# Own PSUM banks for the first k and q, V shifts on VectorE, a first FFN step in token halves, split output tiles and a halved last tile in a fused attention and FFN kernel

## The chip, the cores and the metric

The kernel runs on one core of one Trainium2 chip. The metric is the device time of one execution in microseconds (us), lower is better. The profiled span of one execution is 1.7 to 1.9 us shorter than the time that is reported for the same execution. "PE" is the tensor engine, "DVE" the vector engine, "ACT" the scalar engine, "POOL" is GpSimd, "SP" is SyncE. Work in PSUM is read by DVE or ACT; such a read-out to SBUF is called an eviction here.

## The reference, cut to what matters

```python
# q, k, v: [8 batches, 8 heads, 576 positions, 64], float32
scores = (q @ k.T) / 8, masked to a causal window of 64 positions
attn = softmax(scores) @ v                     # -> x: [4608 tokens, 512]
g = x @ w_gate; val = x @ w_val                # 512 -> 1536
out = (g * sigmoid(g) * val) @ w_out           # 1536 -> 512, float32
```

The 4608 tokens are 36 chunks of 128 for the attention and 9 blocks (c = 0 to 8) of 512 for the FFN. One FFN block is 12 groups F(c, f) (eight matmuls of 512 columns each) and 4 output tiles O(c, u) (twelve matmuls each).

## The kernel before: the parts that matter

A small recording layer takes the operations in program order and puts one semaphore wait where two engines depend on each other. Each engine runs its own operations strictly in program order. PSUM has eight banks: 0 to 3 for the FFN groups, 4 for output tiles, 5 to 7 for everything of the attention.

For chunks 4 to 11, k and q are transposed on PE and evicted by DVE and ACT (for later chunks a DMA transposes them):

```python
def T(self, n):
    ...                                # one bank: k in its first half, q in its second
    g.op("pe", pe, ..., writes=[bk])   # 8 transposes 128x128
    g.op("dve", lambda e: e.tensor_copy(kd, tb[:, 0]), reads=[bk], writes=[kT..., (bk, "k")])
    g.op("act", lambda e: e.activation(qz[0:64, :, 0, :], tb[0:64, 1], ACTF.Copy),
         reads=[bk, (bk, "k")], ...)   # low heads of q; waits for the k copy: same bank
    g.op("dve", lambda e: e.tensor_copy(qz[64:128, :, 1, :], tb[64:128, 1]), reads=[bk], ...)
```

An FFN group, which needs both ACT and DVE:

```python
def F(self, c, f):
    G, gk = self.bank("f"); V, vk = self.bank("f")
    g.op("pe", mm(G, self.Wg), ...)
    g.op("act", lambda e: e.activation(sig, G, ACTF.Tanh, scale=0.5), ...)     # 0.60 us
    g.op("pe", mm(V, self.Wv), ...)
    g.op("dve", ... uu = (sig + 1) * G ...)                                    # 0.69 us
    g.op("dve", ... hT = 0.5 * uu * V ...)                                     # 0.69 us
```

The program order of the first blocks, cut:

```python
self.first_loads(); self.init(); self.load_v(0); ...; W(0, 1); ...   # weights after V
self.first_casts(0); ...; self.first_T(0); self.first_T(1); ...      # chunks 0 to 3
for n in range(4):
    self.Sx(n, 1, True); self.AV(n, 0)       # scores + exp; attention output
for n in range(4):
    self.AV(n, 1)
    if n > 0: self.X(n - 1, "act")           # transpose of x, evicted by ACT
self.X(3, "act")
load(4); load(5); self.load_wo(0, 6); self.load_wo(6, 12)
for f in range(6): self.F(0, f)
self.T(4); self.F(0, 6); self.Sx(4, 0); self.F(0, 7); self.Sx(4, 1); self.T(5) ...
```

The softmax here doesn't subtract the row's maximum and nothing guards it: scores larger than these inputs give would overflow.

## Time and profile before

355.31 us, the median of 3 runs (354.79 to 355.55); the profiled span is 353.6 us.

| stage (boundaries on PE) | us | PE busy | DVE busy | what paces it |
|---|---|---|---|---|
| prologue, to the first FFN matmul | 25.83 | 12.45 | 17.49 | waits between PE, DVE and ACT |
| F(0,0) to F(0,5) | 10.4 | 10.2 | 7.2 | PE |
| T(4) to the first output tile | 16.01 | 14.50 | 14.21 | see below |
| output tiles of block 0 | 16.15 | 15.07 | 9.22 | short waits |
| FFN block 1 | 29.30 | 27.22 | 25.43 | see below |
| the rest | 255.9 | 249.2 | 153.6 | PE, full |

The first two lines of the page give the span and each engine's busy time with its share:

```profile
span 353.6 us, 6112 instructions
PE 328.6 (93%) x2298; PEld 173.1 (49%) x2336; DVE 227.1 (64%) x484; ACT 140.8 (40%) x236; POOL 123.9 (35%) x163
```

The view of waits, PE alone. Each line: who waited, for what, us in total, how often, the longest. These are idle times of PE as the profile counts them, from the modelled end of the matmul before:

```profile
PE ps L316 <- ACT c L306: 7.6, 1, 7.6
PE ps L424 <- DVE nmask L274: 3.1, 1, 3.1
PE ps L509 <- DVE xT L484: 1.9, 2, 1.4
PE ps L532 <- DVE hT L519: 1.3, 1, 1.3
...
PE ps L532 <- DVE rc L462: 1.0, 1, 1.0
PE ps L509 <- ACT xT L486: 0.9, 1, 0.9
```

The reader sees a prologue that waits for the first cast (L306) and for `nmask` (a tile of large negative numbers that a matmul adds to the first scores to mask them), a wait at the end of FFN block 1 (`xT`), and one before the very last output tiles (`hT`, the tanh and the two DVE steps of the last group).

The windows view gives busy us (and number of instructions) of each engine in a stretch; the two stretches are "T(4) to the first output tile" and "FFN block 1":

```profile
core 0: us, PE busy (x) PEld busy (x) DVE busy (x) ACT busy (x) POOL busy (x), PEclk, DMA share, GB/s
36.21:52.22 16.01, 14.50 (x123) 8.19 (x125) 14.21 (x31) 6.92 (x12) 5.87 (x7) 1.00 1.81 188
68.37:97.67 29.30, 27.22 (x220) 14.99 (x225) 25.43 (x56) 12.89 (x22) 15.14 (x19) 1.00 1.50 152
```

DVE is busy 89% and 87% of these stretches, ACT 43% and 44%. The timeline of DVE around T(4) says something more exact (start, length, what, and the idle time before it with what ended it):

```profile
36.88 0.69 DVE L519 SCALAR_TENSOR_TENSOR hT<-uu,ps 128x512 bf16<-128x512 bf16 x1
37.49 0.42 DVE L387 COPY kT<-ps 128x512 bf16<-128x512 bf16 x1
37.94 0.43 DVE L390 COPY qz<-ps 64x512 bf16<-64x512 bf16 x1
39.05 0.69 DVE L517 SCALAR_TENSOR_TENSOR uu<-sig,ps 128x512 bf16<-128x512 bf16 x1 [0.68 <-ACT sig L515]
```

And ACT at the same time:

```profile
37.94 0.59 ACT L388 ACTIVATE qz<-ps 64x512 bf16<-64x512 bf16 x1 [1.81 <-DVE kT L387]
38.43 0.58 ACT L515 ACTIVATE sig<-ps 128x512 bf16<-128x512 f32 x1
```

ACT first waits 1.81 us for DVE's k copy, then evicts its half of q, then does the tanh, and DVE idles 0.68 us for that tanh.

### The profile page before, as it was taken

To read this page: it belongs to the slowest core of one execution; us is meant where nothing else is said; L and a number is where in the kernel's file an instruction comes from. 1 tells how busy PE (TensorE), PEld (TensorE's weight loads), DVE (VectorE), ACT (ScalarE), POOL (GpSimd) and SP (SyncE) were. 2 spreads that over 40 slices of the span, in tenths; PEclk is the share of its full clock that TensorE was granted. 3 is DMA by queue.
4 is the path that set the end of the run, shared out by engine and by line. 5 is a ranking of instruction groups with operands and counts; after the bars stand their busy time and mean duration, and the time that the engine had idled before them with its cause. 6 is when DMAs were issued, how large, how long until landed. Compare 5 with 4: busy or idle time off the path is not lost.

```text
span 353.6 us, 6112 instructions
## 1 busy us (share of the span) xinstructions
PE 328.6 (93%) x2298; PEld 173.1 (49%) x2336; DVE 227.1 (64%) x484; ACT 140.8 (40%) x236; POOL 123.9 (35%) x163
## 2 busy tenths in 40 slices
PE   1669989999899999999999999999999999999985
PEld 1654545555445555554555455545555555444432
DVE  6677795488956666666666666666666666655510
ACT  2463535454434444444444444444444444232222
POOL 8985517835643245424331437243100000000000
PEclk9999999999999999999999999999999999999999
DMA  8999999999989999999999999999944411100012
GB/s 238 195 208 172 219 160 209 196 165 156 126 62 149 162 157 152 153 158 154 156 153 159 162 141 155 154 152 150 170 117 113 104 45 46 45 30 32 30 59 89
DMA packets 178045, 48.17 MB, mean 136 GB/s; under 512 B 160160, under 2 KB 173408, under 8 KB 178016
## 3 DMA queue, kind: packets, MB, share of 16 engines
q0 software_dynamic: 113584, 17.84, 70.6%
q1 hardware_dynamic: 63376, 28.90, 41.0%
q10 hardware_dynamic: 1056, 1.05, 0.9%
q8 instruction: 18, 0.29, 0.3%
q14 instruction: 11, 0.09, 0.1%
HBM read 37.75 MB, written 9.44 MB: 133 GB/s over the span
## 4 chain that ended last, share of the span: by engine, by line
PE 75%; DVE 16%; DMA 3%; ACT 3%; issue 1%
PE ps L509 41%; PE ps L532 25%; DVE hT L519 5%; DVE uu L517 4%; PE ps L425 4%; DVE xb L465 2%; DMA xT<-xb 2%; PE ps L456 2%; PE ps L455 2%; DMA f<-in_q_dram 2%; ACT sig L515 1%; DVE pt L443 1%; PE ps L316 1%; DVE xT L484 1%; PE ps L424 1%
## 5 line engine op out<-in xcount | busy, mean ns | idle before, releaser
L517 DVE SCALAR_TENSOR_TENSOR uu<-sig,ps 128x512 bf16<-128x512 bf16 x108 | 74.1, 686 | 91.3 <-ACT sig L515 91.3
L509 PE MATMUL ps<-xT,Wg 128*128 128x512 bf16 x423 | 109.1, 379 | 3.7 <-DVE xT L484 1.9
L509 PE MATMUL ps<-xT,Wv 128*128 128x512 bf16 x432 | 110.9, 379 | 0.0
L532 PE MATMUL ps<-Wo,hT 128*128 128x512 bf16 x403 | 92.9, 379 | 3.8 <-DVE hT L519 1.3
L515 ACT ACTIVATE sig<-ps 128x512 bf16<-128x512 f32 x108 | 64.4, 596 | 68.2 <-PE ps L509 68.2
L519 DVE SCALAR_TENSOR_TENSOR hT<-uu,ps 128x512 bf16<-128x512 bf16 x108 | 74.2, 687 | 3.7
L509 PEld LDWEIGHTS ps<-xT,Wv 128*128 128x128 bf16 x432 | 42.3, 98 | 51.0
L532 PEld LDWEIGHTS ps<-Wo,hT 128*128 128x128 bf16 x432 | 40.9, 98 | 46.9 <-DVE hT L519 2.7
L509 PEld LDWEIGHTS ps<-xT,Wg 128*128 128x128 bf16 x432 | 39.9, 98 | 45.0 <-DVE xT L484 2.3
L437 ACT ACTIVATE pt<-ps 128x512 bf16<-128x512 f32 x72 | 42.9, 596 | 43.3 <-PE ps L425 42.6
L342 POOL DMA_DIRECT2D va<-in_v_dram x40 | 34.1, 859 | 71.6 <-PE ps L425 69.7
L537 ACT ACTIVATE ost<-ps 128x512 f32<-128x512 f32 x36 | 21.5, 597 | 74.8 <-PE ps L532 74.8
L291 POOL DMA_DIRECT2D qd<-in_q_dram x54 | 39.0, 736 | 28.0 <-DMA qz<-qd 28.0
L291 POOL DMA_DIRECT2D kn<-in_k_dram x36 | 31.0, 868 | 12.4 <-PE ps L382 11.1
L465 DVE TENSOR_TENSOR xb<-ps,rc 128x256 bf16<-128x256 f32 x72 | 30.6, 425 | 2.5
L425 PE MATMUL ps<-qz,kT 128*128 128x128 bf16 x288 | 30.5, 223 | 1.0 <-DVE xb L465 0.3
L443 DVE TENSOR_TENSOR pt<-pt,mask 128x512 bf16<-128x512 bf16 x64 | 26.6, 416 | 1.5 <-ACT pt L437 1.4
L456 PE MATMUL ps<-va,pt 128*128 128x65 bf16 x288 | 26.9, 193 | 0.0
L455 PE MATMUL ps<-vb,pt 128*128 128x65 bf16 x288 | 26.9, 193 | 0.1
L455 PEld LDWEIGHTS ps<-vb,pt 128*128 128x128 bf16 x288 | 22.6, 98 | 7.3 <-DVE xT L484 0.2
L456 PEld LDWEIGHTS ps<-va,pt 128*128 128x128 bf16 x288 | 20.2, 98 | 7.1
L425 PEld LDWEIGHTS ps<-qz,kT 128*128 128x128 bf16 x288 | 19.1, 99 | 2.6 <-DVE qz L390 1.1
(46 smaller groups left out, 106.8 us busy)
## 6 DMA issues: line engine op xcount, KB each, us to landing
out_dram<-ost SPq DMA_DIRECT2D x36, 256.0 KB, 2.7
vb<-va SPq DMA_DIRECT2D x71, 80.0 KB, 3.1
va<-in_v_dram POOLq DMA_DIRECT2D x32, 128.0 KB, 4.4
kn<-in_k_dram POOLq DMA_DIRECT2D x28, 128.0 KB, 6.2
qd<-in_q_dram POOLq DMA_DIRECT2D x42, 64.0 KB, 4.1
Wo<-in_moe_w_out_dram POOLq DMA_DIRECT2D x2, 768.0 KB, 18.7
Wg<-in_moe_w_gate_dram POOLq DMA_DIRECT2D x5, 256.0 KB, 12.5
Wv<-in_moe_w_val_dram POOLq DMA_DIRECT2D x5, 256.0 KB, 12.9
```

Source lines behind the costliest of these rows:

```text
L291: self.g.op("pool", lambda e, d=d, a=az: e.dma_start(d, a), writes=kz, dma=True)
L342: g.op("pool", lambda e, d=d, a=a: e.dma_start(d, a), writes=ks, dma=True)
L425: r = e.matmul(sv[:, w, c], self.kT[:, pr, k0:k0 + 128], qz[:, pr, :, 64 * w:64 * w + 64], start=not bias, stop=True)
L437: g.op("act", lambda e: e.activation(po, si, ACTF.Exp, scale=SCALE), reads=[bk], writes=[pk])
L455: e.matmul(av[:, j, :], pt[:, h, 0:128], vb[:, h, 0:65], start=True, stop=False)
L456: r = e.matmul(av[:, j, :], pt[:, h, 64:192], va[:, h, 0:65], start=False, stop=True)
L465: g.op("dve", lambda e: e.tensor_tensor(xo, av[:, :, 0:64], rb, ALU.mult), reads=[bk, ("rc", ir)], writes=[("xb", ix, half)])
L509: r = e.matmul(bank[:, :], W[:, kk, f * 128:f * 128 + 128], xT[:, kk, :], start=(kk == 0), stop=(kk == NK - 1))
L515: g.op("act", lambda e: e.activation(sig[:, :], G[:, :], ACTF.Tanh, scale=0.5), reads=[gk], writes=[("sig", i)])
L517: g.op("dve", lambda e: e.scalar_tensor_tensor(uu[:, :], sig[:, :], 1.0, G[:, :], ALU.add, ALU.mult), reads=[("sig", i), gk], writes=[("uu ...
L519: g.op("dve", lambda e: e.scalar_tensor_tensor(hT[:, f, :], uu[:, :], 0.5, V[:, :], ALU.mult, ALU.mult), reads=[("uu", i), vk], writes=[(" ...
L532: r = e.matmul(OB[:, :], hT[:, f, 128 * u:128 * u + 128], self.Wo[:, f, :], start=(f == 0), stop=(f == NF - 1))
```

## The change

Intent: warm the PE clock and shorten the prologue, take evictions and memsets off DVE, let PE work during the waits for x, and shorten the end. The diff, cut to its core (the recorded `F2` runs F(0,0) and F(0,1) on tokens 0 to 255 and then on 256 to 511; `O(..., mid)` runs `mid` after 8 of 12 matmuls; `O_last` makes the last tile in two halves of 256 columns, evicted by ACT and DVE; `first_vb` is a "V shift", which copies one half of a chunk's V to the other 64 partitions, tile `vb`, on DVE or, with "sp", by DMA):

```diff
+        self.warm(13)                       # matmuls on zeros, whose results nobody reads
-        self.first_T(0); self.first_T(1)    # k and q of a head pair in one bank
+        self.first_T("k", 0); self.first_T("q", 0); self.warm(8)   # k and q in own banks
-        self.init_nmask()                   # DVE, from mask
+        self.init_mask(self.nmask, "nmask", -30000.0)              # POOL
+        self.first_vb(0, 1, "dve"); self.first_vb(0, 0, "dve"); self.first_vb(1, 1, "dve")
+        for n, part in ((1, 0), (2, 1), (2, 0), (3, 1), (3, 0)): self.first_vb(n, part, "sp")
...
+        self.F2(0, 0)
         self.X(2, "act"); self.X(3, "act")
+        self.F2(0, 1)
-        for f in range(6):
+        for f in range(2, 6):
             self.F(0, f)
...  # in T(n), chunks 4 to 11:
-        g.op("dve", lambda e: e.tensor_copy(qz[64:128, :, 1, :], tb[64:128, 1]), reads=[bk], ...)
+        g.op("act", lambda e: e.activation(qz[64:128, :, 1, :], tb[64:128, 1], ACTF.Copy), reads=[bk, (bk, "k")], ...)
...
-        self.X(4)                           # x evictions of chunks 4 to 11: DVE
+        self.X(4, "act")
-        self.O(0, 2); self.X(6); self.AV(7, 0); self.Sx(8, 0)
+        self.O(0, 2, mid)                   # mid: X(6), AV(7, 0), Sx(8, 0)
...
+                if late: self.O(c - 1, u)   # last block: output tile after the last F
-        for u in range(4): self.O(NFC - 1, u)
+        for u in range(3): self.O(NFC - 1, u)
+        self.O_last(NFC - 1, 3)
```

More of the change, by code (lines that the diff above doesn't have):

```diff
@@ L191, in alloc @@
         self.nmask = sb("nmask", 4 * 64)
+        self.wz = sb("wz", 512)
         self.pt = [t[:, :].rearrange("p (h x) -> p h x", h=H) for t in ring("pt", self.NP, H * 192)]
@@ L225, in init @@
         ident, mask = self.ident, self.mask
+        g.op("dve", lambda e: e.memset(self.wz[:, :], 0.0), writes=["wz"])
         g.op("dve", lambda e: e.memset(ident[:, :], 0.0), writes=["ident"])
+        g.op("dve", lambda e: e.memset(self.nmask[:, :], 0.0), writes=["nmask"])
         g.op("dve", lambda e: e.memset(mask[:, :], 1.0), writes=["mask"])
@@ L246, in init_qd, with init_va @@
                 d = self.qd[i][:, :, e_, 64 - 64 * e_:128 - 64 * e_]
-                self.g.op("dve", lambda e, d=d: e.memset(d, 0.0), writes=[("qd", i, 0), ("qd", i, 1)])
-    def init_va(self, i0):
+                self.g.op("pool", lambda e, d=d: e.memset(d, 0.0), writes=[("qd", i, 0), ("qd", i, 1)])
+    def init_va(self, i0, eng="dve"):
         g = self.g
@@ L252, in init_va @@
             va = self.va[i]
-            g.op("dve", lambda e, va=va: e.memset(va[:, :, 64:80], 1.0), writes=[("va", i)])
+            g.op(eng, lambda e, va=va: e.memset(va[:, :, 64:80], 1.0), writes=[("va", i)])
     def init_pool_a(self):
@@ L259, in init_pool_a, with init_mask @@
             pattern=[[-1, 128]], channel_multiplier=1), writes=["ident"])
-    def init_pool_b(self):
-        m = self.mask
+    def init_mask(self, m, key, fill):
         mm = m[:, :].rearrange("p (a q) -> p a q", a=4)
         self.g.op("pool", lambda e: e.affine_select(
-            out=mm, in_=mm, compare_op=ALU.is_gt, fill=0.0, base=0,
-            pattern=[[0, 4], [-1, 64]], channel_multiplier=1), writes=["mask"])
+            out=mm, in_=mm, compare_op=ALU.is_gt, fill=fill, base=0,
+            pattern=[[0, 4], [-1, 64]], channel_multiplier=1), writes=[key])
         self.g.op("pool", lambda e: e.affine_select(
-            out=mm, in_=mm, compare_op=ALU.is_ge, fill=0.0, base=64,
-            pattern=[[0, 4], [1, 64]], channel_multiplier=-1), writes=["mask"])
-        self.g.op("pool", lambda e: e.memset(m[0:64, 128:192], 0.0), writes=["mask"])
-    def init_nmask(self):
-        m = self.mask
-        self.g.op("dve", lambda e: e.tensor_scalar(self.nmask[:, :], m[:, :], -1.0, 30000.0, ALU.add, ALU.mult),
-                  reads=["mask"], writes=["nmask"])
+            out=mm, in_=mm, compare_op=ALU.is_ge, fill=fill, base=64,
+            pattern=[[0, 4], [1, 64]], channel_multiplier=-1), writes=[key])
+        self.g.op("pool", lambda e: e.memset(m[0:64, 128:192], fill), writes=[key])
     def load_qk(self, n):
@@ L299, in first_loads, with first_cast @@
                 self.g.op(eng, lambda e, d=d, a=a: e.dma_start(d, a), writes=[(nm, half)], dma=True)
-    def first_casts(self, half):
+    def first_cast(self, which, half):
         hs = slice(4 * half, 4 * half + 4)
-        ck = self.ck[:, :, hs].rearrange("p j h d -> p h j d")
-        cq = self.cq[:, :, hs].rearrange("p j h d -> p h j d")
-        self.g.op("dve", lambda e: e.tensor_copy(ck, self.fk[:, hs]), reads=[("fk", half)], writes=[("ck", half)])
-        self.g.op("act", lambda e: e.activation(cq, self.fq[:, hs], ACTF.Copy), reads=[("fq", half)], writes=[("cq", half)])
@@ L308, in first_T, with first_vb @@
-    def first_T(self, pr):
+        dst, src, eng = (self.ck, self.fk, "dve") if which == "k" else (self.cq, self.fq, "act")
+        d = dst[:, :, hs].rearrange("p j h d -> p h j d")
+        rk, wk = [("f" + which, half)], [("c" + which, half)]
+        if eng == "dve":
+            self.g.op("dve", lambda e: e.tensor_copy(d, src[:, hs]), reads=rk, writes=wk)
+        else:
+            self.g.op("act", lambda e: e.activation(d, src[:, hs], ACTF.Copy), reads=rk, writes=wk)
+    def first_vb(self, n, part, eng):
+        i = n + 1 - part
+        dst = self.vb[i][64:128] if part else self.vb[i][0:64]
+        src = self.va[n][0:64] if part else self.va[n][64:128]
+        rd, wr = [("va", n, 0), ("va", n, 1), ("va", n)], [("vb", i, part)]
+        if eng == "dve":
+            self.g.op("dve", lambda e: e.tensor_copy(dst, src), reads=rd, writes=wr)
+        else:
+            self.g.op("sp", lambda e: e.dma_start(dst, src), reads=rd, writes=wr, dma=True)
@@ L309, in first_T @@
+    def first_T(self, which, half, hi="dve"):
         g = self.g
         bank, bk = self.bank("a")
-        tb = bank[:, :].bitcast(BF).rearrange("p (w j t) -> p w j t", w=2, j=4)
+        tb = bank[:, :].bitcast(BF).rearrange("p (c j t) -> p c j t", c=2, j=4)
+        src = self.ck if which == "k" else self.cq
         def pe(e):
-            for w, src in ((0, self.ck), (1, self.cq)):
+            for c in range(2):
+                pr = 2 * half + c
                 for j in range(4):
-                    r = e.transpose(tb[:, w, j, :], src[:, j, 2 * pr:2 * pr + 2, :], self.ident[:, :])
+                    r = e.transpose(tb[:, c, j, :], src[:, j, 2 * pr:2 * pr + 2, :], self.ident[:, :])
@@ L317, in pe @@
             return r
-        g.op("pe", pe, reads=["ident", ("ck", pr // 2), ("cq", pr // 2)], writes=[bk])
-        kd = self.kT[:, pr, 64:576].rearrange("p (t j) -> p t j", j=4)
-        kk = [("kT", n, pr) for n in range(4)]
-        g.op("dve", lambda e: e.tensor_copy(kd, tb[:, 0].rearrange("p j t -> p t j")), reads=[bk], writes=kk + [(bk, "k")])
-        for e_, eng in ((0, "act"), (1, "dve")):
-            ps = slice(64 * e_, 64 * e_ + 64)
-            d = self.qza[ps, :, pr, e_, :].rearrange("p r (t j) -> p r t j", j=4)
-            a = tb[ps, 1].rearrange("p j (r t) -> p r t j", r=4)
-            zk = [("qz", n, pr, e_) for n in range(4)]
-            if eng == "act":
-                g.op("act", lambda e, d=d, a=a: e.activation(d, a, ACTF.Copy), reads=[bk, (bk, "k")], writes=zk)
-            else:
-                g.op("dve", lambda e, d=d, a=a: e.tensor_copy(d, a), reads=[bk], writes=zk)
+        g.op("pe", pe, reads=["ident", ("c" + which, half)], writes=[bk])
@@ new lines, in first_T, with ev @@
+        prs = slice(2 * half, 2 * half + 2)
+        if which == "k":
+            kd = self.kT[:, prs, 64:576].rearrange("p c (t j) -> p c t j", j=4)
+            ks = tb.rearrange("p c j t -> p c t j")
+            kk = [("kT", n, p) for n in range(4) for p in (2 * half, 2 * half + 1)]
+            g.op("dve", lambda e: e.tensor_copy(kd, ks), reads=[bk], writes=kk)
+            return
+        for e_, eng in ((0, "act"), (1, hi)):
+            ps = slice(64 * e_, 64 * e_ + 64)
+            zk = [("qz", n, p, e_) for n in range(4) for p in (2 * half, 2 * half + 1)]
+            def ev(e, ps=ps, e_=e_, eng=eng):
+                for c in range(2):
+                    d = self.qza[ps, :, 2 * half + c, e_, :].rearrange("p r (t j) -> p r t j", j=4)
+                    a = tb[ps, c].rearrange("p j (r t) -> p r t j", r=4)
+                    r = e.activation(d, a, ACTF.Copy) if eng == "act" else e.tensor_copy(d, a)
+                return r
+            g.op(eng, ev, reads=[bk], writes=zk)
@@ L333, in load_v, with warm, pe @@
+    def warm(self, count):
+        bank, bk = self.ps[7], ("ps", 7)
+        def pe(e):
+            for _ in range(count):
+                r = e.matmul(bank[:, :], self.wz[:, 0:128], self.wz[:, :], start=True, stop=True)
+            return r
+        self.g.op("pe", pe, reads=["wz"], writes=[bk])
     def load_v(self, n, copy=True):
@@ L389, in T @@
              reads=[bk, (bk, "k")], writes=[("qz", iz, p, 0) for p in range(4)])
-        g.op("dve", lambda e: e.tensor_copy(qz[64:128, :, 1, :], tb[64:128, 1]), reads=[bk], writes=[("qz", iz, p, 1) for p in range(4)])
+        g.op("act", lambda e: e.activation(qz[64:128, :, 1, :], tb[64:128, 1], ACTF.Copy), reads=[bk, (bk, "k")], writes=[("qz", iz, p, 1) for p in range(4)])
     def TD(self, n):
@@ L520, in F, with F2, pe, gate @@
              reads=[("uu", i), vk], writes=[("hT", ih, f)])
-    def O(self, c, u):
+    def F2(self, c, part):
+        g = self.g
+        it = c % self.NX
+        xT = self.xT[it]
+        ts = slice(256 * part, 256 * part + 256)
+        xk = [("xT", it, 2 * part), ("xT", it, 2 * part + 1)]
+        if part == 0:
+            self.f2 = [self.bank("f") for _ in range(4)]
+        for i, (bank, bk) in enumerate(self.f2):
+            f, W, wk = i // 2, (self.Wg, self.Wv)[i % 2], ("Wg", "Wv")[i % 2]
+            def pe(e, bank=bank, f=f, W=W):
+                for kk in range(NK):
+                    r = e.matmul(bank[:, ts], W[:, kk, f * 128:f * 128 + 128], xT[:, kk, ts],
+                                 start=(kk == 0), stop=(kk == NK - 1))
+                return r
+            g.op("pe", pe, reads=xk + [(wk, f)] + ([(bk, "half")] if part else []), writes=[(bk, "half"), bk])
+        if part == 0:
+            return
+        for f in range(2):
+            i = self.n_s % self.NS
+            self.n_s += 1
+            self.gate(c, f, i, *self.f2[2 * f], *self.f2[2 * f + 1])
+    def gate(self, c, f, i, G, gk, V, vk):
+        g = self.g
+        ih = c % self.NH
+        hT, sig, uu = self.hT[ih], self.sig[i], self.uu[i]
+        g.op("act", lambda e: e.activation(sig[:, :], G[:, :], ACTF.Tanh, scale=0.5), reads=[gk], writes=[("sig", i)])
+        g.op("dve", lambda e: e.scalar_tensor_tensor(uu[:, :], sig[:, :], 1.0, G[:, :], ALU.add, ALU.mult),
+             reads=[("sig", i), gk], writes=[("uu", i)])
+        g.op("dve", lambda e: e.scalar_tensor_tensor(hT[:, f, :], uu[:, :], 0.5, V[:, :], ALU.mult, ALU.mult),
+             reads=[("uu", i), vk], writes=[("hT", ih, f)])
+    def O(self, c, u, mid=None):
         g = self.g
@@ L528, in O, with part, pe @@
         OB, ok = self.bank("o")
-        def pe(e):
-            for f in range(NF):
-                r = e.matmul(OB[:, :], hT[:, f, 128 * u:128 * u + 128], self.Wo[:, f, :],
-                             start=(f == 0), stop=(f == NF - 1))
-            return r
-        g.op("pe", pe, reads=[("hT", ih, f) for f in range(NF)] + [("Wo", f) for f in range(NF)], writes=[ok])
+        def part(f0, f1):
+            def pe(e):
+                for f in range(f0, f1):
+                    r = e.matmul(OB[:, :], hT[:, f, 128 * u:128 * u + 128], self.Wo[:, f, :],
+                                 start=(f == 0), stop=(f == NF - 1))
+                return r
+            g.op("pe", pe, reads=[("hT", ih, f) for f in range(f0, f1)] + [("Wo", f) for f in range(f0, f1)], writes=[ok])
+        if mid is None:
+            part(0, NF)
+        else:
+            part(0, 8)
+            mid()
+            part(8, NF)
         g.op("act", lambda e: e.activation(ost[:, :], OB[:, :], ACTF.Copy), reads=[ok], writes=[("ost", io)])
@@ L539, in O, with O_last, pe @@
         g.op("sp", lambda e: e.dma_start(self.out[r0:r0 + 128, :], ost[:, :]), reads=[("ost", io)], dma=True)
+    def O_last(self, c, u):
+        g = self.g
+        ih = c % self.NH
+        hT = self.hT[ih]
+        ost = self.ost[(4 * c + u) % self.NO]
+        io = (4 * c + u) % self.NO
+        r0 = 512 * c + 128 * u
+        for w, eng in ((0, "act"), (1, "dve")):
+            OB, ok = self.bank("o")
+            cs = slice(256 * w, 256 * w + 256)
+            def pe(e, OB=OB, cs=cs):
+                for f in range(NF):
+                    r = e.matmul(OB[:, 0:256], hT[:, f, 128 * u:128 * u + 128], self.Wo[:, f, cs],
+                                 start=(f == 0), stop=(f == NF - 1))
+                return r
+            g.op("pe", pe, reads=[("hT", ih, f) for f in range(NF)] + [("Wo", f) for f in range(NF)], writes=[ok])
+            d, a = ost[:, cs], OB[:, 0:256]
+            if eng == "act":
+                g.op("act", lambda e, d=d, a=a: e.activation(d, a, ACTF.Copy), reads=[ok], writes=[("ost", io), ("osth", w)])
+            else:
+                g.op("dve", lambda e, d=d, a=a: e.tensor_copy(d, a), reads=[ok, ("ost", io)], writes=[("osth", w)])
+            q = "sp" if w == 0 else "act"
+            g.op(q, lambda e, d=d, cs=cs: e.dma_start(self.out[r0:r0 + 128, cs], d), reads=[("osth", w)], dma=True)
     def S(self, n):
@@ L558, in build @@
         self.init()
-        self.load_v(0)
+        self.load_v(0, False)
         self.init_pool_a()
-        self.load_v(1)
-        self.init_pool_b()
-        self.load_v(2)
-        self.load_v(3)
+        self.init_mask(self.nmask, "nmask", -30000.0)
+        for n in range(1, 4):
+            self.load_v(n, False)
         W(0, 1)
         W(1, 2)
+        self.init_mask(self.mask, "mask", 0.0)
         for f in range(2, 12, 2):
@@ L570, in build @@
         self.banks("a", [5, 6, 7, 4, 0, 1, 2, 3])
-        self.first_casts(0)
+        self.warm(13)
         self.init_pt()
-        self.first_T(0)
-        self.first_T(1)
-        self.first_casts(1)
-        self.init_nmask()
+        self.first_cast("k", 0)
+        self.first_cast("q", 0)
+        self.first_T("k", 0)
+        self.first_T("q", 0)
+        self.warm(8)
+        self.first_cast("k", 1)
+        self.first_cast("q", 1)
+        self.first_vb(0, 1, "dve")
+        self.first_vb(0, 0, "dve")
+        for n, part in ((1, 0), (2, 1), (2, 0), (3, 1), (3, 0)):
+            self.first_vb(n, part, "sp")
+        self.first_T("k", 1)
+        self.first_vb(1, 1, "dve")
         self.Sx(0, 0, True)
         self.Sx(1, 0, True)
-        self.first_T(2)
+        self.first_T("q", 1)
         self.Sx(2, 0, True)
-        self.first_T(3)
         self.Sx(3, 0, True)
-        for n in range(4):
+        self.AV(0, 0)
+        self.Sx(0, 1, True)
+        self.AV(1, 0)
+        for n in range(1, 4):
             self.Sx(n, 1, True)
-            self.AV(n, 0)
-        for n in range(4):
-            self.AV(n, 1)
-            if n > 0:
-                self.X(n - 1, "act")
+        self.AV(0, 1)
+        self.AV(1, 1)
+        self.X(0, "act")
+        self.AV(2, 0)
+        self.AV(2, 1)
+        self.X(1, "act")
+        self.AV(3, 0)
+        self.AV(3, 1)
+        self.banks("a", [5, 6, 7])
+        self.F2(0, 0)
+        self.X(2, "act")
         self.X(3, "act")
-        self.banks("a", [5, 6, 7])
-        self.init_va(4)
-        self.init_qd()
+        self.F2(0, 1)
+        self.init_va(4, "pool")
         load(4)
@@ L620, in build @@
         self.T(6)
+        self.init_qd()
         load(8)
         self.O(0, 0)
-        self.X(5)
+        self.X(5, "act")
         self.Sx(6, 0)
@@ L633, in build, with mid @@
         self.T(8)
-        self.O(0, 2)
-        self.X(6)
-        self.AV(7, 0)
-        self.Sx(8, 0)
+        def mid():
+            self.X(6, "act")
+            self.AV(7, 0)
+            self.Sx(8, 0)
+        self.O(0, 2, mid)
         self.AV(7, 1)
@@ L640, in build @@
         self.T(9)
-        self.O(0, 3)
-        self.X(7)
+        self.O(0, 3, lambda: self.X(7, "act"))
         load(10)
@@ L649, in build @@
                 load(n + 4, False)
+                last = u == 3
+                late = c == NFC - 1 and last
                 self.F(c, 3 * u)
@@ L652, in build @@
                     self.AV(n, 0)
+                    if last:
+                        self.AV(n, 1)
                     if n + 1 < NCH:
@@ L658, in build @@
                 if live:
-                    self.AV(n, 1)
+                    if not last:
+                        self.AV(n, 1)
                     if n + 1 < NCH:
                         self.Sx(n + 1, 1)
-                if live and c > 1:
-                    self.XD(n)
+                if live:
+                    if c > 1:
+                        self.XD(n)
+                    elif last:
+                        self.X(n, "act")
                     if n + 3 < NCH:
                         self.copy_v(n + 3)
-                if c > 1:
+                if c > 1 and not late:
                     self.O(c - 1, u)
                 self.F(c, 3 * u + 2)
-                if live and c == 1:
-                    self.X(n)
-                    self.copy_v(n + 3)
-                if n + 2 < NCH and n + 2 < self.ND:
+                if live and c == 1 and not last:
+                    self.X(n, "act")
+                if n + 2 < self.ND:
                     self.T(n + 2)
+                if late:
+                    self.O(c - 1, u)
         self.banks("o", [0, 1, 2, 3])
-        for u in range(4):
+        for u in range(3):
             self.O(NFC - 1, u)
+        self.O_last(NFC - 1, 3)
         self.g.emit()
```

## The prediction

> **What bounds it now.** Span 353.6 us. From 97.6 us on the tensor engine is full: matmuls of 512 columns start every 0.216 us, one 128-token step takes 8.7 us, exactly its work. The slack stands in five places.
>
> 1. Prologue (timeline): first FFN matmul at 25.83 us. PE waits 7.6 us for the q cast, 3.1 for `nmask` (queued on DVE behind four evictions and a cast), 0.8 for `qz`, 0.8 for `xb`, 0.9 for `xT`. Matmuls of 128 columns start 0.107 us apart until 17.4 us, then 0.056. The Trainium skill, "TensorE: Matmul & The Clock Gate", Part 1, says the array starts at half rate until about 3.4 us of sustained work; the trace agrees in kind (4.8 us).
> 2. First FFN token block, 25.8 to 52.2 us: DVE busy 14.0 of 15.8 us from 36.4 on (windows); the chain of waits runs over it.
> 3. First output tiles, 52.2 to 68.4: 16.15 us for about 14.7 of PE work, waiting on `xb` and x evictions.
> 4. Second block, 68.4 to 97.6: DVE busy 25.4 of 29.2; PE work about 26.2.
> 5. End: 1.27 us before the last output tiles, then 0.60 eviction and about 2.7 DMA.
>
> **What changes, costed.**
> - Prologue: zero matmuls warm the clock from about 1.3 us; k and q halves get own banks; `nmask` moves to POOL and no longer queues on DVE; three V shifts move from DMA (5.3 us from issue to landing) to DVE. Scores start about 11.7 (12.6), second-half scores about 15 (18.6), ACT exponentials end about 18.3 (21.9). With the first FFN step split by tokens, F(0,2) starts at about 24.6 instead of 29.3: 4.7 us won.
> - **Part is given back.** Loads on the POOL-issued queue land in order, and are queued 14 us deep: the k rows of chunk 4 land at 33.25 us, behind the weights. Their transposes, now at 36.2, would be reached at 31.5 and must wait until about 33.4. About 3 us survive. Chunk 6 lands at 47.0 (transposed at 50.6): a second ceiling, 3.6 us.
> - The high q eviction (0.69) and x eviction (0.43) leave DVE for ACT (under half busy). First block from T(4): DVE 14.0 becomes about 12, PE work 13.4: about 0.7 us won, limited by chunk 6.
> - Output tiles split: about 1 us. Second block loses 3.1 us of DVE work and becomes PE-bound: 29.2 to about 27, 2.3 us won.
> - The c=8 output tile after the last FFN step hides the 1.27 us; half-tile end about 0.3; attention before x transposes about 0.4.
>
> Sum on the critical path: 3 + 0.7 + 1 + 2.3 + 2 = 9 us, discounted to 8.5.
>
> **Prediction: 346.8 us, 8 in 10 between 343.0 and 350.5.** Faster by over 2% (below 348.2): 0.68; within 2%: 0.31; slower: 0.01.
>
> **What would show it.** Timeline: dense 0.056 us spacing at the first scores; no PE wait on `nmask`; F(0,2) near 24.6; T(4) preceded by a PE wait of about 2 us ended by the DMA of chunk 4's k, at about 33.4; second block near 27 us with DVE busy under 24; no 1.27 us gap before the last tiles.
>
> **What would make it wrong.** The queue draining faster once DMA shifts are gone; the zero matmuls not warming the clock; V shifts on DVE slow or waiting for V (landing 10.3 to 12.8 us); ACT becoming the limit through in-order evictions; POOL memsets delaying load issue.

## The result and the profile after

The changed kernel took 351.61 us (median of 4 runs, 350.69 to 352.67) against 355.43 us of before on the same chip. All ratios in this text are the mean time of one kernel's fast runs over that of the other's in the same rounds, so not quite the ratio of the medians quoted; here 0.9896, 95% interval 0.9864 to 0.9929. A repeat on another chip gave 350.27 us and 0.9839 (below, run after_again). So the change gains 1.0 to 1.6%, and lands within 2%, not at the 346.8 us predicted.

The page after:

```profile
span 348.8 us, 6255 instructions
PE 335.0 (96%) x2385; PEld 175.4 (50%) x2385; DVE 220.4 (63%) x461; ACT 149.2 (43%) x252; POOL 127.3 (37%) x176
```

Where the 4.8 us of span came from, by milestones that both programs share (start times in us from the ACT and DVE timelines; two later experiments are put beside them):

| milestone | before | after | t_hi_dve | best |
|---|---|---|---|---|
| tanh of F(0,2) | 30.35 | 27.39 | 27.02 | 25.89 |
| k copy of chunk 4 | 37.49 | 34.53 | 34.16 | 33.03 |
| eviction of the first output tile | 54.79 | 53.09 | 51.24 | 50.22 |
| tanh of F(1,0) | 69.44 | 67.61 | 65.10 | 64.08 |
| tanh of F(2,0) | 98.74 | 96.14 | 92.15 | 91.15 |
| tanh of F(8,8) | 329.70 | 327.13 | 323.19 | 321.74 |
| end | 353.6 | 348.8 | 344.9 | 343.4 |

Differences of neighbouring rows, before minus after: prologue +2.96; to chunk 4's k copy 0; from there to the first output tile **-1.26**; output tiles +0.13; block 1 +0.77; blocks 2 to 8 -0.03; end +2.23; together 4.80. The prologue and the end gained what was predicted. The stages in the middle, where DVE work had been removed, gained next to nothing or lost. Each column is one trace, but the stages repeat well: in the five traces that share these stages with the changed kernel (after, no_f2, no_warm, vb_dma, end_undo) the stretch from the k copy to the first output tile takes 18.56 to 18.58 us and block 1 takes 28.53 to 28.55. The prologue repeats less well: F(0,2) is at 27.4 us in two traces of it and at 27.0 in four.

PE's waits after (line numbers are now those of the changed kernel: L416 is the k copy of T, L417 and L419 its low and high q evictions, L454 the scores, L538, L544, L546 and L548 the matmuls, tanh and two DVE steps of F, L564 the matmuls of F2, L328 the first transposes, L357 the zero matmuls):

```profile
PE ps L454 <- ACT qz L419: 2.1, 4, 0.8
PE ps L357 <- DVE wz L227: 1.3, 1, 1.3
PE ps L328 <- DVE c L304: 1.2, 1, 1.2
PE ps L453 <- DVE qz L347: 1.1, 1, 1.1
PE ps L564 <- ACT xT L515: 1.0, 1, 1.0
PE ps L564 <- DVE xb L494: 0.9, 1, 0.9
PE ps L538 <- DMA xT<-xb: 0.8, 1, 0.8
```

The `nmask` wait and the 1.3 us wait before the last tiles are gone. On top stands a wait that did not exist: scores (L454) wait for `qz L419`, which is exactly the moved eviction of q's high heads. Further down stand the two token halves of F2 (L564), waiting for DVE and ACT.

The same two windows (T(4) to the first output tile; block 1):

```profile
33.23:50.29 17.06, 14.65 (x125) 8.06 (x124) 12.92 (x27) 8.71 (x15) 8.18 (x16) 1.00 1.81 189
66.53:95.07 28.54, 27.29 (x224) 14.97 (x225) 21.96 (x49) 16.93 (x29) 15.58 (x20) 1.00 1.68 161
```

In the first stretch DVE does 1.3 us less work and the stretch is 1.05 us longer. DVE's throughput was not its limit. (The two block 1 windows do not cut DVE's work at the same place: from tanh to tanh, F(1,0) to F(2,0), DVE's work falls from 25.43 to 23.00 us, 56 to 50 instructions.) The DVE timeline around T(4):

```profile
33.92 0.69 DVE L548 SCALAR_TENSOR_TENSOR hT<-uu,ps 128x512 bf16<-128x512 bf16 x1
34.53 0.42 DVE L416 COPY kT<-ps 128x512 bf16<-128x512 bf16 x1
36.83 0.69 DVE L546 SCALAR_TENSOR_TENSOR uu<-sig,ps 128x512 bf16<-128x512 bf16 x1 [1.88 <-ACT sig L544]
```

And ACT:

```profile
34.98 0.59 ACT L417 ACTIVATE qz<-ps 64x512 bf16<-64x512 bf16 x1 [1.82 <-DVE kT L416]
35.58 0.59 ACT L419 ACTIVATE qz<-ps 64x512 bf16<-64x512 bf16 x1
36.20 0.60 ACT L544 ACTIVATE sig<-ps 128x512 bf16<-128x512 f32 x1
```

ACT still waits 1.82 us for the k copy, then evicts both halves of q in series, and only then does the tanh. DVE now idles 1.88 us instead of 0.68. From k copy to the next `uu` it was 1.56 us (37.49 to 39.05), now it is 2.30 us: 0.74 us more. The same step from 0.68 to 1.88 us of idle DVE stands at five of the eight transposes: four that a tanh follows (chunks 4, 5, 10 and 11), and chunk 7, where an exponential follows.

The wait for the k copy is not there for data: ACT reads q, DVE reads k, but both lie in one bank. The Trainium skill, "PSUM — Partial Sum Buffer", section "PSUM bank collisions raise a hardware error", says that two engines may not access the same bank and 32-partition quadrant at once, reads against reads included, and that the hardware does not arbitrate. No run here shows a collision. The run t_two takes the wait away by another bank instead.

### The profile page after: what moved, and what is told of

Read it like the earlier page. It is cut to its first block, busy times and chain, and to the rows that moved or that the text cites. A ratio compares the mean times of both kernels' runs of the same rounds, so it can differ in the third digit from the quotient of the medians.

```text
span 348.8 us, 6255 instructions
## 1 busy us (share of the span) xinstructions
PE 335.0 (96%) x2385; PEld 175.4 (50%) x2385; DVE 220.4 (63%) x461; ACT 149.2 (43%) x252; POOL 127.3 (37%) x176
## 4 chain that ended last, share of the span: by engine, by line
PE 79%; DVE 12%; ACT 5%; DMA 2%; issue 1%
PE ps L538 45%; PE ps L597 23%; PE ps L454 4%; DVE hT L548 3%; DVE uu L546 2%; PE ps L485 2%; PE ps L484 2%; PE ps L357 2%; DMA xT<-xb 2%; DVE xb L494 2%; DVE pt L472 1%; ACT sig L544 1%; ACT qz L419 1%; ACT qz L417 1%; PE ps L564 1%
## 5 line engine op out<-in xcount | busy, mean ns | idle before, releaser
L546 DVE SCALAR_TENSOR_TENSOR uu<-sig,ps 128x512 bf16<-128x512 bf16 x106 | 72.5, 684 | 92.5 <-ACT sig L544 92.2
L538 PE MATMUL ps<-xT,Wg 128*128 128x512 bf16 x424 | 108.8, 379 | 1.0 <-DMA xT<-xb 0.8
L538 PE MATMUL ps<-xT,Wv 128*128 128x512 bf16 x424 | 108.8, 379 | 0.0
L597 PE MATMUL ps<-Wo,hT 128*128 128x512 bf16 x420 | 96.2, 379 | 0.6 <-DVE hT L548 0.6
L544 ACT ACTIVATE sig<-ps 128x512 bf16<-128x512 f32 x106 | 63.3, 597 | 61.5 <-PE ps L538 61.4
L548 DVE SCALAR_TENSOR_TENSOR hT<-uu,ps 128x512 bf16<-128x512 bf16 x106 | 72.8, 686 | 3.7
L538 PEld LDWEIGHTS ps<-xT,Wv 128*128 128x128 bf16 x424 | 41.5, 98 | 50.0 <-DVE hT L583 0.2
L597 PEld LDWEIGHTS ps<-Wo,hT 128*128 128x128 bf16 x420 | 39.8, 98 | 43.5 <-DVE hT L548 0.7
L538 PEld LDWEIGHTS ps<-xT,Wg 128*128 128x128 bf16 x424 | 39.4, 98 | 41.9 <-DMA xT<-xb 1.3
L454 PE MATMUL ps<-qz,kT 128*128 128x128 bf16 x288 | 28.8, 219 | 3.3 <-ACT qz L419 2.1
L484 PE MATMUL ps<-vb,pt 128*128 128x65 bf16 x288 | 25.8, 193 | 0.1
L485 PE MATMUL ps<-va,pt 128*128 128x65 bf16 x288 | 25.9, 193 | 0.0
L454 PEld LDWEIGHTS ps<-qz,kT 128*128 128x128 bf16 x288 | 18.7, 97 | 6.6 <-ACT qz L419 3.1
```

The source lines that it names most:

```text
L454: r = e.matmul(sv[:, w, c], self.kT[:, pr, k0:k0 + 128], qz[:, pr, :, 64 * w:64 * w + 64], start=not bias, stop=True)
L484: e.matmul(av[:, j, :], pt[:, h, 0:128], vb[:, h, 0:65], start=True, stop=False)
L485: r = e.matmul(av[:, j, :], pt[:, h, 64:192], va[:, h, 0:65], start=False, stop=True)
L538: r = e.matmul(bank[:, :], W[:, kk, f * 128:f * 128 + 128], xT[:, kk, :], start=(kk == 0), stop=(kk == NK - 1))
L544: g.op("act", lambda e: e.activation(sig[:, :], G[:, :], ACTF.Tanh, scale=0.5), reads=[gk], writes=[("sig", i)])
L546: g.op("dve", lambda e: e.scalar_tensor_tensor(uu[:, :], sig[:, :], 1.0, G[:, :], ALU.add, ALU.mult), reads=[("sig", i), gk], writes=[("uu ...
```

## The experiments

Theory A: the moved q eviction lengthens the chain k copy, q eviction, q eviction, tanh, and so delays the FFN step that DVE waits for. Rival B: the x evictions moved to ACT do that. Rival C, the prediction's own: DVE throughput bounds these blocks, and the loss is elsewhere. Further runs test the parts of the prologue and of the end. The medians of before on the three chips used were 355.64 to 355.74 us. The control was run on one of these chips, with t_hi_dve, x_dve and t_two. The other runs come from two other chips (no_f2, no_warm, pro_fix and pro_fix_early on one; best, vb_dma, end_undo and both_dve on the other), and the control itself differs by 1.3 us between its two measurements. So a time that is set against the control from another chip is only a hint where it differs by 1 to 3 us; there the stages of the traces decide.

### after_again: the control

The changed kernel, unedited.

> The changed kernel unedited, as the control on this chip. All theories: near 351.6 us (350.7 to 352.7). It also tells whether the 0.96 us wait for an x transpose by DMA at 130 us in the first profile comes back (then it belongs to the kernel) or not (then it is scatter of the DMA).

Measured: 350.27 us (ratio 0.9839, 0.9805 to 0.9872) over its five fast runs and one slow one of 359.75 us with a granted clock of 0.949. The slow one was the profiled one, so no stage is read from it, and whether the wait at 130 us returns could not be told from it; eight other variants show a wait of 0.3 to 1.7 us at that block start, while t_hi_dve and no_f2 list none, so it is not confined to one profile, but its size differs from profile to profile. The control was 1.3 us better than the first measurement of the same kernel.

### t_hi_dve: undo only the moved q eviction

```diff
-        g.op("act", lambda e: e.activation(qz[64:128, :, 1, :], tb[64:128, 1], ACTF.Copy), reads=[bk, (bk, "k")], ...)
+        g.op("dve", lambda e: e.tensor_copy(qz[64:128, :, 1, :], tb[64:128, 1]), reads=[bk], ...)
```

> Only the high q eviction of chunks 4 to 11 goes back from ACT to DVE. Theory A (eviction chain: DVE k copy 0.42, then ACT 0.59, then ACT 0.59, and only then the tanh that the next FFN group waits for): DVE idle after each k copy falls from 1.88 to about 0.7 us, and each of the 8 transposes gives back 0.7 to 0.9 us net of the 0.43 us of DVE work, so the kernel gets 3 to 5 us faster than the control, about 347.5. Theory B (x evictions on ACT are what delays tanh) expects no more than 1 us. Theory C (DVE throughput bounds these blocks, as the prediction had it): 8 x 0.43 = 3.4 us slower.

Measured: 346.87 us (346.14 to 347.80), ratio to before 0.9747 (0.9716 to 0.9779). That is 3.4 us faster than the control on the same chip, from one line, and the fast runs of the two do not overlap. Its DVE timeline around T(4):

```profile
34.16 0.42 DVE L416 COPY kT<-ps 128x512 bf16<-128x512 bf16 x1
34.61 0.43 DVE L419 COPY qz<-ps 64x512 bf16<-64x512 bf16 x1
35.71 0.69 DVE L546 SCALAR_TENSOR_TENSOR uu<-sig,ps 128x512 bf16<-128x512 bf16 x1 [0.68 <-ACT sig L544]
```

And its two windows:

```profile
33.22:48.44 15.22, 14.36 (x122) 8.17 (x125) 13.43 (x29) 7.52 (x13) 8.23 (x16) 1.00 1.74 193
64.03:91.08 27.05, 26.65 (x221) 14.90 (x225) 22.82 (x51) 15.77 (x27) 15.98 (x20) 1.00 1.85 185
```

The idle time is back to 0.68 us. DVE does more work than in the changed kernel in both stretches, and both are shorter, by 1.84 and 1.49 us. Theory A holds; C predicted the opposite sign.

### x_dve: undo only the moved x evictions

```diff
-        self.X(4, "act")      # and the same for X(5), X(6), X(7) and the X(n) of block 1
+        self.X(4)
```

> Only the x evictions of chunks 4 to 11 go back from ACT to DVE. Theory A: within 1 us of the control. Theory B: 2 us or more faster than the control. Theory C (DVE throughput): about 8 x 0.43 = 3.4 us slower, or what part of it lies in the DVE-paced blocks.

Measured: 351.05 us (349.85 to 352.91), ratio 0.9865: 0.8 us slower than the control by the medians, with ranges that overlap. B falls: the x evictions on ACT are not what costs. C's 3.4 us is not there either. In its trace block 1 (tanh of F(1,0) to tanh of F(2,0)) takes 29.45 us against 28.53 in the changed kernel, so this move is worth about 0.9 us in that block. In the output-tile stage it is the other way round: 13.79 us against 14.52.

### both_dve: undo both

```diff
+        t_hi_dve and x_dve together
```

> t_hi_dve with the x evictions of chunks 4 to 11 on DVE too. DVE throughput (the prediction's reason for moving them): up to 8 x 0.43 us slower than t_hi_dve's 346.9, so 348 or more. Chain theory: what counts is which engine the next tanh or FFN step waits on, so within 1 us, 346.5 to 347.8.

Measured: 347.48 us (346.56 to 349.58), ratio 0.9769. Against t_hi_dve, on another chip, that is 0.6 us slower by the medians with overlapping ranges. In the trace block 1 takes 27.98 us against 27.05, again 0.9 us, and the output-tile stage 13.42 against 13.86. So in both pairs the x eviction on ACT is a small gain on balance (0.4 and 0.95 us from chunk 4's k copy to the tanh of F(2,0)), and the q eviction on ACT a loss of 3.4 us on one chip, and 3.6 us between runs of two chips.

This run shows one thing more. Here are the windows of block 1, tanh to tanh, first of before and then of both_dve:

```profile
69.44:98.74 29.30, 27.22 (x221) 14.99 (x224) 25.43 (x56) 12.89 (x22) 14.07 (x18) 1.00 1.49 152
65.22:93.20 27.98, 27.22 (x221) 14.89 (x224) 25.24 (x56) 12.89 (x22) 14.91 (x19) 1.00 1.86 181
```

DVE does the same work, 25.2 to 25.4 us, and the block is 1.32 us shorter. What is gone is the wait of 1.40 us for the last `xT` at the block's end (97.67 us in before): the changed kernel transposes that x earlier. That no run undid this order alone leaves its share unproven, but DVE's throughput, busy 90% here, did not set the length of this block in before.

### t_two: keep the eviction on ACT, take away its wait for the k copy

```diff
-        one bank for k and q; ACT reads=[bk, (bk, "k")]
+        two banks of the ring 5 to 7 for k and q; both ACT evictions reads=[bq] only
```

> k and q of chunks 4 to 11 are transposed into two PSUM banks, both q halves still evicted by ACT, which no longer has to wait for the k copy on DVE (the wait kept two engines off one bank). If most of the cost is the wait for the k copy in its place behind DVE's FFN steps, tanh comes as early as before and 3 us or more come back. If it is the second ACT eviction (0.59 us each), only the wait of about 1.3 to 1.8 us before the first q eviction goes, and the tanh of the group in flight is no longer late either, since both evictions then end before its matmuls do: then too 3 us or more. If neither, within 1 us of the control, and the loss is elsewhere (banks, loads).

Measured: 348.17 us (347.45 to 351.41), ratio 0.9804 (0.9760 to 0.9849), a verdict of unclear: by the medians 2.1 us of the 3.4 come back, less than the 3 us expected, but two of its six runs (349.81 and 351.41) lie among or above the control's. ACT no longer names DVE as what it waited for at T(4):

```profile
34.06 0.59 ACT L420 ACTIVATE qz<-ps 64x512 bf16<-64x512 bf16 x1 [1.27 <-PE ps L412]
34.66 0.59 ACT L421 ACTIVATE qz<-ps 64x512 bf16<-64x512 bf16 x1
35.28 0.60 ACT L546 ACTIVATE sig<-ps 128x512 bf16<-128x512 f32 x1
```

By stages it is instructive. From chunk 4's k copy to the first output tile it takes 16.80 us and block 1 takes 26.65 us; t_hi_dve takes 17.08 and 27.05. With the wait gone, two evictions on ACT are in these two stages no worse than one on each engine, as the intent of the change was. (The second bank also lets each copy start after four transposes and not eight; two banks with the high half on DVE were not run, so what each part gives is not separated.) But the output-tile stage takes 15.57 us against 13.86: T now takes two of three banks of its ring, and PE's transposes (L412) wait 1.4 us there for DVE and ACT to free banks, as the view of waits for 48 to 67 us shows. So these stages fit a cost that lies in the serial order behind the k copy and not in ACT's work as such, and the second bank has its price where attention work is dense.

### no_f2, no_warm, vb_dma: the parts of the prologue

no_f2 makes the first FFN step whole again:

```diff
-        self.F2(0, 0)
         self.X(2, "act"); self.X(3, "act")
-        self.F2(0, 1)
-        for f in range(2, 6):
+        for f in range(6):
```

> The changed kernel with the first FFN step whole again (F(0,0) and F(0,1) after all four x transposes). x of chunk 3 is in place about 23.2 us (xb at 21.3, transpose, ACT), so F starts near 23.0 and F(0,2) near 26.5 instead of 26.3. If the token halves are worth what I gave them, F(0,2) is 1.5 us later than in the changed kernel; if the turn-around between the halves eats them, within 0.4 us. The total follows: within 0.5 us, or 1.5 us slower, than the control's 350.3.

Measured: 350.18 us (ratio 0.9853), the same as the control's 350.27, and the tanh of F(0,2) at 27.02 us (27.39 in the changed kernel, 27.0 in four variants with the same prologue). The token halves are worth nothing that these runs can show. The first half waits for banks 0 and 1, which still hold chunk 3's attention outputs, and the second waits for x evictions that could start only after the first half had left PE. Here are PE's lines of the changed kernel:

```profile
20.86 0.61 PE L564 MATMUL ps<-xT,Wg 128*128 128x256 bf16 x4 [0.88 <-DVE xb L494]
...
24.29 0.61 PE L564 MATMUL ps<-xT,Wg 128*128 128x256 bf16 x4 [0.95 <-ACT xT L515]
```

(From start to start, without the modelled tails of matmuls, these two gaps are the 1.04 and 1.12 us that the expectation of pro_fix names.)

no_warm leaves out the 21 matmuls on zeros.

```diff
-        self.warm(13)
-        self.warm(8)
```

> The changed kernel without its 21 matmuls on zeros. If they hold the clock up: 128-column matmuls start 0.107 us apart for about 4 us of the prologue, costing 0.3 us at the first k transposes and about 0.5 us more before the first scores; F(0,2) later by 0.5 to 1.5 us. If the zero matmuls are off the path (transposes and scores wait for DVE and ACT anyway): within 0.3 us of the changed kernel in the timeline, and in the total.

Measured: 351.59 us (351.33 to 352.06), ratio 0.9889: 1.3 us slower than the control, but the same as the first measurement of the changed kernel (351.61), so the time alone shows nothing. The trace does: the tanh of F(0,2) comes at 28.56 us, 1.17 later than in the changed kernel's trace, and the stages after it are as long as there (18.57, 14.53 and 28.54 us). The zero matmuls pay. PE's first lines without them:

```profile
7.02 1.89 PE L328 MATMUL ps<-ident,c 128*128 128x128 bf16 x16 [7.02 <-DVE c L304]
11.40 1.03 PE L328 MATMUL ps<-ident,c 128*128 128x128 bf16 x8 [2.49 <-DVE c L304]
```

And with them, in the changed kernel:

```profile
1.26 5.73 PE L357 MATMUL ps<-wz 128*128 128x512 bf16 x13 [1.26 <-DVE wz L227]
7.01 1.13 PE L328 MATMUL ps<-ident,c 128*128 128x128 bf16 x16
```

The 16 transposes shrink from 1.89 to 1.13 us. The Trainium skill, "TensorE: Matmul & The Clock Gate", Part 1, gives a time budget of about 3.4 us of activity and a free-running window. Without the zero matmuls, scores start 0.107 us apart from 12.2 to 15.6 us, 3.4 us, and 0.056 afterwards; but transposes at the same slow pace lead straight into them from 11.4, and counted from there it is 4.2 us. With them, the slow pace ends 5.9 us after the first zero matmul in this trace (at 7.2 us), and between 2.8 and 5.9 us after it in the eleven fast traces that have them. So the budget is no constant here; that the window runs freely fits this spread.

vb_dma puts the three V shifts back on the DMA queue:

```diff
-        self.first_vb(0, 1, "dve"); self.first_vb(0, 0, "dve"); self.first_vb(1, 1, "dve")
+        the same shifts with "sp"
```

> The changed kernel with the three V shifts back on the DMA queue. Shifts take 5.3 us from issue to landing, V of chunk 0 lands at 10.2: chunk 0's shifts land near 15.7 to 16.5, so its first attention output (13.7 us in the changed kernel) waits about 2.5 us, and all eight shifts land about 1.5 us later. DVE saves 1.57 us before the second-half q eviction, so the second-half scores start 1.2 to 1.5 us earlier. Shifts matter: F(0,2) 1 to 2 us later, total 351.3 to 352.3. Shifts do not matter (ACT's exponentials are the pace): within 0.5 us of the control.

Measured: 353.05 us (351.93 to 353.45), ratio 0.9916: 2.8 us slower than the control, which was on another chip, and 1.4 slower than the first measurement of the changed kernel; its trace is 2.4 us longer than the changed kernel's. The 1 to 2 us expected lie at the lower end of this. In its trace the shifts of chunk 0 land at 15.7 and 16.7 us, and PE waits for them:

```profile
PE ps L484 <- DMA vb<-va: 2.5, 2, 2.0
```

The tanh of F(0,2) comes 1.56 us later, as expected; about 0.7 us more is lost between the tanh of F(2,0) and that of F(8,8), where waits for x transposes by DMA sum to 1.2 us (0.8 in the changed kernel).

### pro_fix and pro_fix_early: is there a load ceiling at chunk 4?

The prediction said that chunk 4's transposes would be stopped by the landing of its k. In the changed kernel they were not: its k landed at 33.06 us and the transposes started at 33.23 with no wait, because the prologue had come out slower than I had walked it. In five runs in which F(0,2) came 0.4 us earlier (t_hi_dve, x_dve, both_dve, t_two, no_f2) PE already waits 0.2 to 0.6 us for this load. To find out whether the ceiling exists, pro_fix makes the prologue faster, on top of t_hi_dve:

```diff
+        self.banks("a", [5, 6, 7, 4])                 # before AV(3, 0): off banks 0 and 1
         self.AV(3, 0); self.AV(3, 1)
-        self.F2(0, 0)
-        self.X(2, "act"); self.X(3, "act")
+        self.F2(0, 0, {2: X(2), 3: X(3)})             # before its third and fourth bank
```

> On top of t_hi_dve: chunk 3's attention outputs get banks 5 and 6 instead of the banks 0 and 1 that the first FFN half-step needs, and the x transposes of chunks 2 and 3 stand inside that half-step instead of after it. Both theories: the idle before the first FFN half (1.04 us) and the one between its halves (1.12 us) go, F(0,2) starts about 1.6 us earlier (tanh of f2 near 25.4 instead of 27.0 us). Load ceiling (k of chunk 4 lands at 33.05 us whatever the prologue does): PE waits about 1.5 to 1.9 us at chunk 4's transposes, and the kernel stays within 0.4 us of t_hi_dve's 346.9. No ceiling (my prediction's step was wrong): 345.2, with those transposes at about 31.3 us.

Measured: 347.08 us (346.28 to 348.14), ratio 0.976, no faster than t_hi_dve. The tanh of F(0,2) came at 25.89 us (27.02), and then:

```profile
33.35 0.40 PE L411 MATMUL ps<-ident,kn 128*128 128x128 bf16 x4 [1.45 <-DMA kn<-in_k_dram]
```

The ceiling is there: a gain of 1.1 us in the prologue became a wait of 1.45 us. pro_fix_early moves the loads of chunks 4 and 6 forward in the queue:

```diff
         for f in range(2, 12, 2):
+            if f == 8: self.load_qk(4)
             W(f, f + 2)
...
+        self.load_qk(6)
         self.load_wo(6, 12)
```

> pro_fix with the q and k loads of chunk 4 queued before the last four weight loads, and those of chunk 6 before the second w_out load. Load ceiling: chunk 4's k lands about 3 us earlier (near 28 to 30 us), the wait at its transposes goes, and about 1 us of the 1.6 arrives in the time (the rest is caught by chunk 6 or w_out, near 47 us): 345.5 to 346.2. No ceiling: the same as pro_fix, within 0.4 us.

Measured: 346.62 us (345.67 to 347.81), ratio 0.975. Chunk 4's k lands at 27.7 us, the wait is gone, and the tanh of F(2,0) comes at 90.69 us, 1.55 earlier than in pro_fix. But the time is only 0.5 us better, with overlapping ranges. The rest is lost at two later block starts, where PE waits for the last x transpose of a block by DMA. These are PE's line at the first of them and the sum of such waits in the waits view:

```profile
126.34 0.82 PE L538 MATMUL ps<-xT,Wg 128*128 128x512 bf16 x3 [1.74 <-DMA xT<-xb]
...
PE ps L538 <- DMA xT<-xb: 2.3, 2, 1.7
```

### best: also take those two transposes off the DMA

```diff
-                    if c > 1:
+                    if c > 1 and not (last and c < 4):
                         self.XD(n)                    # else: PE transpose, ACT eviction
```

> pro_fix_early with the x transpose of the last chunk of the second and third attention blocks (chunks 15 and 19) on PE and ACT instead of a DMA that took 4.6 to 6.0 us. If the 1.5 us that pro_fix_early won by 92 us was lost to the waits for these DMAs at 124 and 161 us (1.91 and 0.76 us), both waits go for 0.45 us of PE work, and the time is 344.3 to 345.2 (2 us under pro_fix_early's 346.6). If the loss only moves on to other waits for loads, it stays above 346.

Measured: 344.85 us (344.58 to 345.16), ratio to before 0.9691 (0.9670 to 0.9712), outputs correct. Its profile lists no wait of PE for an x transpose at all. This beats before by 3.1% and the changed kernel's control, on another chip, by 5.4 us. All of it is the changed kernel with one line undone, a better order at F2, six loads moved forward and two transposes moved to PE.

### end_undo: the end alone

```diff
-                late = c == NFC - 1 and last
+                late = False
-        three output tiles, then O_last
+        four output tiles
```

> The changed kernel with the end of before: the third-last output tile group ahead of the last FFN step, last tile whole. The 1.27 us wait before the last tiles comes back, and about 0.7 us of the last eviction and store: 2.0 us slower than the control (352.3), all of it after 326 us in the timeline. If the end gain had another source, within 1 us of the control.

Measured: 352.70 us (351.70 to 353.29), ratio 0.9909: 2.4 us slower than the control, which was on another chip; in the traces the end, from the tanh of F(8,8), takes 23.57 us against 21.67, so 1.9 us of this are the end's. The 1.3 us wait for `hT` is back in its list of waits. The rest is the last store: in before the last eviction starts at 350.13 us and the span ends 3.5 us later; in the changed kernel the last half starts its eviction at 346.15 and the span ends 2.7 us later. The end's part of the prediction was right.

## Why the prediction was wrong, point by point

The predicted 346.8 us lay 4.8 us under the first measurement, and the range (343.0 to 350.5) missed it; the control of 350.27 us lies just inside its upper edge. On the same chips before took 355.4 and 355.7 us, so 3.8 and 5.5 us came of the 8.5 predicted. The failing step is this one: "The high q eviction (0.69) and x eviction (0.43) leave DVE for ACT (under half busy)." The two stages that it was to shorten, the first block from T(4) and block 1, were to gain 3.0 us (0.7 and 2.3) and together lost 0.5.

- **Its size was wrong.** The 0.69 us is the strided copy of the prologue. In chunks 4 to 11 the same eviction took 0.43 us on DVE and 0.59 on ACT, so "3.1 us of DVE work" of block 1 was too much: 2.4 us left it.
- **Its mechanism was wrong.** I read a busy share of 87 to 89% as a throughput limit. The runs showed a chain through both engines: k copy on DVE, q evictions on ACT, tanh on ACT, FFN step on DVE. Putting 0.59 us into that chain to take 0.43 us off an engine made DVE idle 1.88 instead of 0.68 us at five of the eight transposes. Undoing only that gave 3.4 us (t_hi_dve). With it undone, the stages from the first output tile's eviction to the tanh of F(1,0) and from there to that of F(2,0) gain 0.8 and 2.25 us over before, where "about 1 us" and "2.3 us" stood in the prediction; the changed kernel itself gained 0.13 and 0.77. For block 1 this nearness is partly luck: both_dve, with both evictions on DVE as in before, gains 1.32 of the 2.25 there without any DVE work having left.
- **First block from T(4)**: predicted 0.7 us won; measured 1.26 us lost, and 0.22 us won with the eviction undone.
- **Prologue**: "F(0,2) starts at about 24.6" was wrong, it started at 26.3. I gave the bank turn-around before the token halves nothing and the x evictions between them too little; the two gaps are 1.04 and 1.12 us. That "about 3 us survive" came true by accident: the ceiling had not yet been reached.
- **Load ceiling**: right in kind. It was not visible in the changed kernel, where k landed 0.2 us before it was needed, though five later runs touched it; pro_fix reached it and waited 1.45 us.
- **Zero matmuls, V shifts, `nmask`**: right. Without the zero matmuls F(0,2) comes 1.2 us later, without the V shifts on DVE 1.6 us later, and the `nmask` wait is gone from the list.
- **End**: predicted about 1.6 us for the reordered tile and the half tiles; the end stage gained 2.23 us. Right in mechanism.
- **"Attention before x transposes about 0.4"** in the full stretch: it did not appear; blocks 2 to 8 took 0.03 us longer. Where it may have paid is block 1 (see both_dve). In the full stretch the DMA transposes still make PE wait at block starts, by amounts that differ between profiles.
- **The listed risk** "ACT becoming the limit through in-order evictions" was the one that came nearest to what happened, and I had given it too little weight in the range.

What stays open: why the x transposes by DMA take 4.6 to 6.0 us at some block starts and 2.3 us in the late blocks. That loads share the DMA engines then fits the fact that they are short once the loads have ended, but no run varied the loads alone. It is also open how much better T with two banks would do if it were used only in FFN blocks.

## What to carry to other kernels

A high busy share does not show that an engine's throughput is the limit: look at what ends its idle times, and if it is the engine to which you want to move work, the move lengthens the chain. Before moving an eviction, ask what stands behind it in the receiving engine's order, and whether it must queue behind another reader of the same bank. When a prologue gets faster, check what lands when, since a queue of loads sets the next floor.

## What the Trainium skill lacked or had wrong

- "TensorE: Matmul & The Clock Gate", Part 4 (PE-mode transpose), says that the full-rate clock does not engage for transposes. Here transposes that follow other matmuls run at full rate: after the zero matmuls, eight of them start 0.056 us apart (0.45 us for eight, 12.39 to 12.84 us of the changed kernel). No run here shows whether transposes alone would bring the clock up: in no_warm the first 16 run about 0.107 us apart, but for 1.6 us only, and the next 8 lead straight into scores.
- The same page, Part 1, gives about 3.4 us of sustained work before the clock rises. Here the slow pace lasted 4.2 us in no_warm, 4.8 us in before, and in the eleven fast traces with zero matmuls 2.8 to 5.9 us from the first of them. The page says that the window runs freely, which fits; a plan needs the larger number.
- "DMA: Bandwidth & Descriptors" gives a bandwidth for DMA transposes but no latency for them; the skill has a time for a single 128x128 tile on another page, but none for a larger one or under load. A transpose of 128x512 bf16 took 2.3 us from issue to landing late in these programs and up to 6.0 us while loads were running.
- The same page, section "Two DMAs through the same engine are not ordered", promises no order of completion. In these traces POOL's loads of the first 34 us landed in the order of issue, up to 15.4 us after it. That is an observation, not a promise, but a plan of what lands when needs it.
- The pages give overheads and rates of DVE and ACT on PSUM, but none sets side by side what one whole eviction takes on each engine: 64x512 bf16 from PSUM took 0.43 us on DVE and 0.59 on ACT, and 0.65 to 0.69 us on DVE with a strided destination.
